# One step for each score tile, squares and scalings that VectorE may take, and another written order, in a fused attention and feed-forward kernel

## The chip, the cores and the metric

The program runs on one core of a Trainium2 chip. The time is the device time of one execution in microseconds (us); the median of three runs of the kernel before is 430.78 us. PE is TensorE, DVE is VectorE, ACT is ScalarE, POOL is GpSimd, and SP is SyncE, whose queue starts most of the transfers.

## The reference, cut to what matters

```python
# q, k, v: (8, 12, 448, 64); w_in: (768, 2048); w_out: (2048, 768)
q_n, k_n = rmsnorm(q, g_q), rmsnorm(k, g_k)          # over the last axis, 64 long
scores = matmul(q_n, k_n.T) / sqrt(64)
attn   = exp(scores - max);  attn = attn / (sum(attn) + 1e-9)
x      = matmul(attn, v)      # heads side by side: (8*448, 768)
h      = x @ w_in
g      = h * clip(h + 3, 0, 6) / 6
out    = g @ w_out            # (3584, 768)
```

## The kernel before, in words

**Units.** The work of the attention is cut into 48 pairs P of two heads, six pairs for each of the 8 batches. A pair goes through these steps. `load` fetches q, k and v of the pair, 256 KB each, by three transfers in SP's queue. `prep` squares q and k (`f_sq`, line 401 on ACT, line 403 on POOL), sums the squares (`f_red`, line 410, DVE), makes the inverse root out of a logarithm and an exponential (`f_ln` and `f_ex`, lines 415 and 418, ACT), scales q and k with it into bf16 (`f_sc`, line 427) and casts v (`f_v`, lines 345 to 351). `trans` transposes the scaled q and k, in PE for the pairs below 13 (line 479) and by a DMA transpose from SP's queue for the rest (line 455). `score` multiplies q by k (line 510), and ACT takes the exponential of a score tile out of PSUM (`f_e`, line 519). `av` multiplies by v (line 531), `finish` divides by the sums (lines 547 and 550) and turns the result into a piece of `xT`, in PE for batches 0 and 1 (line 566) and by a DMA transpose for the rest (line 557).

The feed-forward part has for each batch 16 groups `h` of six matmuls with `w_in` (line 587), each of which needs all six pairs of its batch, an ACT step (line 594) and a DVE step (line 597). For two batches together it has seven groups `y` of 32 matmuls with `w_out` (line 618), evacuated by ACT or DVE and stored. The first two `h` groups of batch 0 are cut into six parts of one matmul each, one part for each pair; every other `h` group is two parts of three. A half of a `y` group is four parts of four matmuls, and part n reads the n-th quarter of `w_out`.

**Score tiles.** A pair has four score tiles of 112 rows by 2 x 448. One tile is two matmuls with 64 rows of weights each, one for each head, and they lie in different halves of the array's rows. There are three places in PSUM for score tiles: `S0` and `S1` in turn, and `X`, which is used for it (the flag `wide`) in pairs from 24 on. `av` accumulates in `X` as well. The two banks `M0` and `M1` serve the `h` and `y` groups.

**Order.** Every step is first recorded in a `Plan` with the engines that could run it. `WAY` names, by step number, which of these engines is taken (0 where nothing stands). The steps are then written out in the order of the list `ORDER`, and `em` ties each instruction to the one before it on its engine. So each engine, and each queue of transfers, runs its steps in exactly that order: a step that waits holds up everything behind it on the same engine. The numbers of time and load in `plan.add` and the values `want` and `since` do not reach the chip; only `WAY` and `ORDER` do.

Before the change one `score` step held the tiles of a group: one tile for pairs below 6, two tiles for pairs 6 to 23, and three, two and three tiles for two pairs from 24 on. A group's matmuls cannot be parted by other work:

```python
def f_s(_):
    for P, t, ps, _ in parts:
        ...
plan.add(pe(0.2 + 0.19 * len(parts)), want, f_s, sorted(reads), [p[3] for p in parts], soon=soon)
```

The squares could be taken by POOL or ACT; the scalings were DVE's for pair 0 and POOL's for the other 47 pairs. The weights are fetched by POOL's queue, four transfers for `w_in` (line 653) and four for `w_out` (line 658), 768 KB each in the type that is stored.

At the start, 120 matmuls on zeros (line 356) keep PE running, and three small ones (line 536) follow each `av` step of the first six pairs.

Of the kernel before, what the change touches and what calls it, by code (L numbers as in the profile page):

```python
# [10 lines left out]
A_MULT = mybir.AluOpType.mult  # L11
# [10 lines left out]
WAY = {53: 1, 63: 2, 67: 1, 68: 1, 69: 1, 78: 1, 83: 1, 84: 1, 95: 1, 101: 1, 126: 1, 132: 2, 157: 1,  # L22
    163: 1, 183: 1, 188: 1, 225: 1, 231: 1, 233: 1, 245: 1, 250: 1, 256: 1, 276: 1, 358: 1, 365: 1, 377: 1,
    388: 1, 400: 1, 424: 2, 429: 1, 446: 1, 453: 1, 458: 1, 460: 1, 487: 1, 500: 1, 505: 1, 516: 1, 518: 1,
    533: 1, 625: 1, 636: 1, 676: 1, 683: 2, 709: 2, 714: 1, 728: 1, 729: 1, 755: 1, 761: 2, 766: 1, 793: 1,
    798: 1, 821: 1, 892: 1, 899: 2, 925: 2, 930: 1, 945: 1, 951: 2, 977: 2, 1003: 2, 1008: 1, 1023: 1,
    1029: 1, 1034: 1, 1061: 1, 1097: 1, 1134: 1, 1148: 1, 1182: 2, 1206: 1, 1212: 1, 1226: 1, 1251: 1,
    1257: 2, 1263: 1, 1398: 1, 1413: 1, 1420: 2, 1426: 1, 1440: 1, 1447: 1, 1453: 1, 1464: 1, 1465: 1,
    1491: 1, 1515: 1, 1516: 1, 1522: 1, 1549: 1, 1555: 1, 1579: 1, 1615: 1, 1620: 1, 1652: 1, 1673: 1,
    1693: 1, 1700: 1, 1706: 1, 1718: 1, 1724: 2, 1744: 1, 1751: 2, 1757: 1, 1781: 1, 1795: 1, 1832: 1,  # L30
    1893: 1, 1921: 1, 1932: 1, 1938: 1, 1958: 1, 1971: 1, 1979: 1, 1980: 1, 1986: 1, 1992: 1, 2057: 1,
    2062: 1, 2093: 1, 2098: 1, 2125: 1, 2145: 1, 2162: 1, 2169: 1}


class Plan:

# [8 lines left out]
    def add(self, ways, want, fn, reads=(), writes=(), load=(), since=0.0, soon=()):  # L49
        i = len(self.ops)  # L50
        self.way[i] = WAY.get(i, 0)
        eng, occ, fin = ways[self.way[i]]
        soon = dict(soon)
        preds = {}

        def after(p, lat):
            preds[p] = max(preds.get(p, 0.0), lat)

        for r in reads:
            if r in self.last:  # L60
                after(*self.last[r])
            self.readers.setdefault(r, []).append((i, fin))
        for w in writes:
            for p in self.readers.get(w, ()):
                if p[0] != i:
                    after(*p)
            if w in self.last:
                after(*self.last[w])
        for w in writes:
            self.last[w] = (i, soon.get(w, fin))  # L70
            self.readers[w] = []
        self.ops.append((eng, occ, fin, want, fn, preds, load, since))
        self.ways.append(ways)
        return i

    def emit(self, order):

        place = {i: n for n, i in enumerate(order)}
        assert len(place) == len(self.ops)
        for i, o in enumerate(self.ops):  # L80
            assert all(place[p] < place[i] for p in o[5])
        for i in order:
            self.ops[i][4](self.ops[i][0])
# [3 lines left out]
    8, 9, 20, 13, 21, 22, 15, 23, 11, 24, 28, 10, 25, 19, 29, 53, 26, 12, 30, 27, 14, 54, 31, 16, 55, 32, 33,  # L87
    34, 17, 58, 35, 56, 36, 83, 37, 92, 38, 78, 59, 39, 60, 40, 57, 62, 41, 18, 69, 42, 43, 44, 61, 45, 93,
    68, 66, 46, 73, 47, 67, 64, 123, 48, 101, 70, 49, 50, 74, 122, 65, 75, 71, 63, 77, 104, 72, 217, 102, 84,
    105, 76, 81, 85, 154, 51, 103, 112, 94, 124, 82, 79, 52, 86, 114, 80, 113, 153, 126, 115, 110, 87, 95,  # L90
    155, 135, 88, 111, 96, 91, 89, 136, 106, 116, 184, 117, 107, 133, 97, 118, 90, 143, 119, 185, 156, 108,
    134, 132, 120, 186, 144, 109, 141, 121, 248, 142, 145, 146, 166, 98, 1, 157, 164, 147, 167, 158, 148, 99,
    165, 174, 163, 149, 215, 137, 150, 159, 172, 100, 125, 387, 138, 151, 175, 127, 0, 139, 216, 173, 218,
    140, 187, 152, 195, 128, 197, 188, 129, 196, 176, 177, 178, 198, 130, 179, 189, 203, 160, 204, 205, 131,
    246, 180, 168, 181, 190, 206, 161, 169, 170, 247, 182, 171, 191, 183, 162, 228, 385, 226, 229, 207, 194,
    208, 386, 201, 227, 199, 192, 209, 416, 202, 210, 200, 236, 211, 234, 225, 212, 237, 230, 414, 219, 213,
    249, 259, 214, 231, 6, 220, 238, 260, 239, 193, 235, 445, 267, 2, 221, 232, 240, 222, 268, 241, 257, 223,
    242, 233, 243, 415, 258, 250, 261, 244, 262, 245, 265, 256, 251, 277, 266, 278, 224, 269, 279, 280, 281,
    443, 252, 396, 388, 253, 397, 263, 270, 271, 264, 255, 272, 398, 285, 286, 273, 287, 274, 288, 254, 289,
    401, 275, 444, 389, 402, 395, 399, 276, 390, 400, 3, 290, 282, 406, 291, 407, 5, 391, 403, 292, 392, 283,  # L100
    472, 405, 394, 297, 284, 298, 404, 393, 293, 299, 408, 294, 417, 502, 300, 425, 295, 418, 305, 426, 296,
    306, 4, 427, 419, 501, 301, 307, 302, 420, 430, 308, 428, 421, 303, 409, 422, 431, 313, 429, 424, 473,
    446, 314, 423, 304, 432, 410, 315, 411, 309, 433, 316, 310, 474, 434, 412, 321, 413, 311, 322, 312, 454,
    323, 531, 447, 435, 455, 436, 324, 317, 456, 448, 318, 329, 319, 503, 475, 459, 449, 457, 320, 450, 437,
    460, 438, 330, 452, 458, 439, 440, 453, 325, 331, 451, 461, 530, 332, 462, 441, 326, 476, 442, 463, 337,
    338, 477, 327, 7, 483, 339, 464, 328, 484, 621, 465, 504, 466, 340, 467, 478, 333, 485, 468, 482, 469,
    486, 345, 479, 487, 480, 488, 346, 489, 470, 622, 534, 490, 347, 471, 491, 334, 348, 481, 493, 492, 494,
    495, 335, 496, 512, 336, 647, 533, 497, 513, 341, 498, 342, 535, 514, 499, 515, 343, 517, 516, 344, 648,
    536, 505, 354, 537, 518, 506, 539, 349, 500, 350, 538, 507, 351, 508, 649, 509, 519, 520, 522, 523, 510,
    355, 521, 356, 511, 524, 541, 544, 625, 525, 542, 526, 527, 543, 357, 699, 540, 352, 358, 635, 624, 528,  # L110
    546, 353, 529, 547, 674, 366, 650, 626, 361, 548, 360, 651, 367, 627, 673, 676, 368, 652, 628, 532, 677,
    549, 632, 700, 633, 550, 630, 678, 551, 552, 369, 634, 629, 553, 362, 679, 554, 675, 370, 637, 653, 545,
    654, 661, 728, 363, 655, 638, 555, 378, 556, 656, 639, 379, 701, 636, 380, 687, 703, 680, 658, 752, 659,
    364, 681, 623, 640, 660, 726, 641, 365, 631, 642, 381, 702, 371, 729, 663, 382, 730, 751, 373, 664, 682,
    374, 665, 704, 375, 731, 889, 732, 684, 662, 705, 727, 685, 561, 643, 686, 562, 644, 645, 376, 706, 372,
    563, 734, 688, 689, 713, 377, 690, 666, 893, 667, 564, 668, 669, 725, 691, 557, 708, 683, 558, 646, 755,
    670, 671, 710, 657, 559, 890, 569, 733, 711, 560, 570, 672, 892, 707, 565, 712, 894, 891, 566, 571, 692,
    739, 693, 567, 694, 572, 695, 895, 915, 715, 896, 568, 716, 577, 696, 709, 578, 753, 717, 573, 383, 714,
    754, 574, 579, 736, 384, 697, 575, 737, 580, 718, 698, 719, 756, 720, 738, 585, 765, 586, 576, 757, 918,
    359, 721, 758, 741, 587, 722, 723, 742, 735, 581, 588, 759, 582, 724, 743, 740, 744, 593, 583, 941, 760,  # L120
    762, 584, 967, 763, 594, 944, 589, 903, 764, 897, 590, 968, 595, 745, 767, 591, 898, 916, 596, 768, 746,
    592, 747, 601, 919, 748, 769, 749, 602, 993, 766, 761, 597, 603, 920, 900, 750, 901, 770, 771, 772, 604,
    969, 773, 902, 598, 774, 775, 994, 970, 609, 921, 599, 899, 610, 922, 776, 924, 600, 905, 611, 908, 906,
    909, 612, 923, 605, 917, 904, 907, 606, 955, 617, 607, 618, 1019, 608, 945, 926, 619, 946, 942, 613, 927,
    910, 943, 911, 928, 620, 614, 996, 912, 929, 781, 947, 913, 948, 615, 997, 931, 925, 1020, 932, 934, 616,
    935, 950, 914, 782, 998, 933, 936, 949, 1021, 777, 783, 937, 999, 784, 778, 1000, 938, 952, 939, 779,
    1146, 1001, 789, 953, 956, 940, 790, 1002, 780, 954, 791, 951, 981, 1148, 971, 785, 1147, 786, 972, 957,
    787, 960, 958, 961, 1197, 788, 792, 1022, 930, 1196, 794, 793, 973, 1149, 959, 795, 1145, 796, 1023, 1150,
# [79 lines left out]
def kernel(  # L208
# [11 lines left out]
    nc = tc.nc  # L220
# [116 lines left out]
    def pool(n, rate):  # L337
        return POOL, 0.02 + n * rate, 0.05 + n * rate
# [443 lines left out]
```

## Time and profile before

| what | value |
|---|---|
| median of three runs | 430.78 us (430.08 to 431.27) |
| span of the profiled execution, first to last instruction | 427.8 us |
| granted TensorE clock | 1.000 |
| PE busy | 415.1 us, 97% |
| ACT, DVE, POOL busy | 296.7, 219.6, 171.1 us |
| transfers | 67.77 MB |

The page gives the span of one execution and not that execution's own time; the median of the runs lies 3.0 us above the span, and this is taken as what lies around it. A row of a group of instructions has the line, the engine, the operation, what is written and read, the shapes and the count; behind the bar stand the busy time in us, the mean of one in ns, and the idle time of the engine just before. A row of the timeline has the start and the length in us, and in brackets how long the engine had been idle and what ended this.

### The profile page before, as it was taken

What the parts mean: (1) busy time and instruction counts of PE and PEld (TensorE: products, weight loads), DVE (VectorE), ACT (ScalarE), POOL (GpSimd) and SP (SyncE); (2) the same over time, 40 slices, a digit from 0 to 9 for tenths busy, and PEclk for the clock granted to TensorE, in tenths of its full rate; (3) what the DMA queues carried; (4) which work ended last, traced back from release to release, by engine and by line L of the source; (5) the groups of instructions that cost most, each with busy time, mean ns of one, the idle gap of its engine ahead of it and who ended that gap; (6) DMA issues with size and microseconds to landing.
All of it is one profiled execution on the core that took longest, in us unless ns stands there. A gap on an engine that the chain in (4) does not pass through costs nothing.

```text
span 427.8 us, 9914 instructions
## 1 busy us (share of the span) xinstructions
PE 415.1 (97%) x3946; PEld 238.6 (56%) x3946; DVE 219.6 (51%) x405; ACT 296.7 (69%) x535; POOL 171.1 (40%) x188
## 2 busy tenths in 40 slices
PE   9678999999999999999999999999999999999996
PEld 8455455555555555555555555555555555655554
DVE  5665776547787965665545454434434332243211
ACT  5999898889998988968757977575575556222221
POOL 2899865874767866255524340312200000000000
PEclk9999999999999999999999999999999999999999
DMA  8999999698799999668565865352413221021113
GB/s 258 349 249 288 242 240 250 149 267 231 197 237 262 229 234 227 187 155 233 136 170 132 215 156 124 75 125 55 93 33 70 50 60 49 11 75 37 38 38 113
DMA packets 98931, 67.77 MB, mean 158 GB/s; under 512 B 53156, under 2 KB 95428, under 8 KB 98884
## 3 DMA queue, kind: packets, MB, share of 16 engines
q1 hardware_dynamic: 93248, 60.50, 54.5%
q0 software_dynamic: 5248, 6.29, 8.4%
q8 instruction: 31, 0.51, 0.5%
q10 hardware_dynamic: 388, 0.34, 0.3%
q14 instruction: 16, 0.13, 0.1%
HBM read 50.23 MB, written 11.01 MB: 143 GB/s over the span
## 4 chain that ended last, share of the span: by engine, by line
PE 90%; ACT 4%; issue 2%; DVE 1%; DMA 1%; POOL 1%; SPq 0%; POOLq 0%
PE M L587 32%; PE M L618 29%; PE X L531 10%; PE S L510 8%; PE S L618 5%; ACT eT L519 2%; PE X L587 1%; DMA qk<-in_k_dram 1%; PE S L587 1%; PE X L510 1%; PE X L618 1%; POOL qks L427 1%; DVE gT L597 0%; SPq L388 0%; ACT ts L594 0%
## 5 line engine op out<-in xcount | busy, mean ns | idle before, releaser
L519 ACT ACTIVATE eT<-S 112x896 bf16<-112x896 f32 x168 | 148.1, 918 | 13.8 <-PE S L510 13.3
L587 PE MATMUL M<-xT,w_in_sb 128*128 128x448 bf16 x714 | 153.2, 353 | 0.8 <-ACT xT L347 0.4
L618 PE MATMUL M<-w_out_sb,gT 128*128 128x384 bf16 x752 | 135.9, 326 | 0.0
L597 DVE SCALAR_TENSOR_TENSOR gT<-ts,M 128x448 bf16<-128x448 f32 x119 | 73.4, 619 | 101.9 <-ACT ts L594 101.7
L427 POOL TENSOR_TENSOR qks<-qk,rs 112x512 bf16<-112x512 f32 x94 | 96.2, 1043 | 65.5 <-DMA T<-qks 31.9
L618 PEld LDWEIGHTS <-gT 128*128 128x128 bf16 x912 | 84.8, 98 | 61.9 <-issue 9.7
L594 ACT ACTIVATE ts<-M 128x448 f32<-128x448 f32 x119 | 64.8, 548 | 61.0 <-PE M L587 59.8
L587 PEld LDWEIGHTS <-w_in_sb 128*128 128x128 bf16 x768 | 69.9, 98 | 65.7 <-issue 10.9
L403 POOL TENSOR_TENSOR sq<-qk 112x512 f32<-112x512 f32 x56 | 57.7, 1041 | 43.4 <-DMA qk<-in_k_dram 18.2
L531 PEld LDWEIGHTS <-eT 112*128 112x128 bf16 x1536 | 57.1, 97 | 18.1 <-issue 8.2
L410 DVE TENSOR_REDUCE ssq<-sq 112x16 f32<-112x1024 f32 (+1 forms) x50 | 57.9, 1172 | 15.8 <-ACT sq L401 11.9
L531 PE MATMUL X<-va,eT 112*128 112x65 bf16 x1536 | 62.3, 194 | 1.0 <-DVE xT L349 0.8
L510 PE MATMUL S<-T 64*128 64x448 bf16 x336 | 47.3, 354 | 2.1 <-ACT eT L519 1.5
L550 DVE TENSOR_TENSOR xn<-X,rd 112x512 bf16<-112x512 f32 x48 | 33.2, 691 | 1.6
L351 POOL CAST va<-vf 112x512 bf16<-112x512 f32 x20 | 12.3, 613 | 41.1 <-PE X L531 38.8
L510 PEld LDWEIGHTS <-T 64*128 64x128 bf16 x384 | 12.8, 94 | 27.9 <-issue 21.0
L401 ACT ACTIVATE sq<-qk 112x512 f32<-112x512 f32 x40 | 24.9, 629 | 4.7 <-DMA qk<-in_q_dram 2.3
L347 ACT COPY y<-M 128x384 f32<-128x384 f32 x26 | 12.5, 481 | 18.4 <-PE M L618 18.1
L547 DVE RECIPROCAL rd<-X 112x8 f32<-112x8 f32 x48 | 9.8, 204 | 28.1 <-PE X L531 27.9
L349 DVE COPY y<-M 128x384 f32<-128x384 f32 x21 | 11.7, 555 | 22.8 <-PE M L618 22.6
L519 ACT ACTIVATE eT<-X 112x896 bf16<-112x896 f32 x24 | 22.1, 923 | 0.0
L618 PE MATMUL S<-w_out_sb,gT 128*128 128x384 bf16 (+1 forms) x128 | 21.8, 316 | 0.0
(58 smaller groups left out, 188.3 us busy)
## 6 DMA issues: line engine op xcount, KB each, us to landing
qk<-in_q_dram SPq DMA_DIRECT2D x47, 256.0 KB, 4.2
qk<-in_k_dram SPq DMA_DIRECT2D x47, 256.0 KB, 4.0
vf<-in_v_dram SPq DMA_DIRECT2D x47, 256.0 KB, 4.8
w_in_sb<-in_moe_w_in_dram POOLq DMA_DIRECT2D x4, 768.0 KB, 12.7
w_out_sb<-in_moe_w_out_dram POOLq DMA_DIRECT2D x4, 768.0 KB, 14.5
out_dram<-y SPq DMA_DIRECT2D x7, 336.0 KB, 2.8
out_dram<-y SPq DMA_DIRECT2D x8, 288.0 KB, 2.7
out_dram<-y SPq DMA_DIRECT2D x8, 240.0 KB, 3.4
```

Of the source, the lines that this page charges most:

```text
L401: em(nc.scalar.square(out=sq[:, i], in_=x))
L403: em(nc.gpsimd.tensor_tensor(out=sq[:, i], in0=x, in1=x, op=A_MULT))
L410: em(nc.vector.tensor_reduce(out=ssq[:, s].rearrange("p i n -> p (i n)"), in_=sq[:, s].rearrange("p i (n d) -> p (i n) d", d=D), axis=AX_X ...
L427: em((nc.vector if e == DVE else nc.gpsimd).tensor_tensor(out=qks[:, i].rearrange("p t h d -> p h t d"), in0=qk[:, i].rearrange("p h (t d) ...
L510: em(nc.tensor.matmul(out=ps[:, a, 0:S], lhsT=qkT[r, S + t * TP:S + t * TP + 128], rhs=qkT[r, 0:S], start=True, stop=True))
L519: em(nc.scalar.activation(out=eT[:, t, 0:S2].rearrange("p (a s) -> p a s", a=2), in_=ps[0:TP, :, 0:S], func=EXP, bias=0.0, scale=1.0))
L531: em(nc.tensor.matmul(out=X_ps[:, a, i * E1:(i + 1) * E1], lhsT=eT[:, t, c:c + 128], rhs=va[:, a, t, :], start=(t == 0 and i == 0), stop=( ...
L550: em(nc.vector.tensor_tensor(out=xn[:].rearrange("p i a d -> p a i d"), in0=xv[:, :, :, 0:D], in1=rd[:].unsqueeze(3).to_broadcast([TP, 2, ...
L587: em(nc.tensor.matmul(out=ps[:, 0:S], lhsT=w_in_sb[:, kt, f * 128:(f + 1) * 128], rhs=xT[:, kt, :], start=(kt == 0), stop=(kt == NKT - 1)))
L594: em(nc.scalar.activation(out=ts[:], in_=ps[:, 0:S], func=RELU, bias=0.5, scale=1.0 / 6.0))
L597: em(nc.vector.scalar_tensor_tensor(out=gT[:, f, e * S:(e + 1) * S], in0=ts[:], scalar=1.0, in1=ps[:, 0:S], op0=A_MIN, op1=A_MULT))
L618: em(nc.tensor.matmul(out=ps[:, 0:nc0], lhsT=gT[:, f, i * 128:(i + 1) * 128], rhs=w_out_sb[:, f, c0:c0 + nc0], start=(f == 0), stop=(f == ...
```

## The change

The kernel computes the same. Four things differ:

- `score` takes one tile, so each of the 192 tiles is a step that can be placed by itself.
- A square may also be taken by DVE, and a scaling by DVE or POOL for any pair. The new `WAY` puts 27 of the 96 squares on DVE (before none), 46 on POOL (56) and 23 on ACT (40); and 41 of the 96 scalings on DVE (2) and 55 on POOL (94). Casts of v, copies and evacuations are handed out anew too: POOL casts v 28 times (20), ACT 8 (12), DVE 12 (16); DVE evacuates `y` 32 times (25), ACT 25 (32).
- `ORDER` is another list throughout.
- The model's numbers in `plan.add` change. They have no effect on the program but through `WAY` and `ORDER`.

```diff
-    def score(slots, want):
-        parts = [(P, t, *((X_ps, ("X",)) if wide else sbank())) for P, t, wide in slots]
+    def score(P, t, wide, want):
+        ps, res = (X_ps, ("X",)) if wide else sbank()
+        qkT, eT, n = T_r[P % NT], eT_r[P % NE], P % NE
...
-        plan.add(pe(0.2 + 0.19 * len(parts)), want, f_s, sorted(reads), [p[3] for p in parts], soon=soon)
...
+        plan.add(pe(0.192), want, f_s, [(("T", P % NT), i) for i in range(2)], [res], half=True)
+        plan.add([act(S2)], want, f_e, [res], [("e", n, t)])
...
-            score(slots, gw)
+            for slot in slots:
+                score(*slot, gw)
...
-                    em(nc.gpsimd.tensor_tensor(out=sq[:, i], in0=x, in1=x, op=A_MULT))
-            plan.add([pool(n, 1.9e-3), act(n, 0.03)][::-1 if P in SQ_ACT else 1], want, f_sq,
+                    em((nc.vector if e == DVE else nc.gpsimd).tensor_tensor(out=sq[:, i], in0=x, in1=x, op=A_MULT))
+            plan.add([pool(n, 1.9e-3), act(n, 0.03)][::-1 if P in SQ_ACT else 1] + [(DVE, 0.62, 0.7)], want, f_sq,
...
-            plan.add([(DVE, 0.75, 0.85) if P == 0 else pool(n, 1.95e-3)], want + 0.01, f_sc,
+            plan.add([(DVE, 0.75, 0.85), pool(n, 1.95e-3)][::1 if P == 0 else -1], want + 0.01, f_sc,
...
-            plan.add([(POOL, 0.8, 3.0)], -20.0, f_o, [], [("w_out", c)], load=(4.8, 150), since=AT_OUT[c])
+            plan.add([(POOL, 0.8, 3.0)], -20.0, f_o, [], [("w_out", c)], load=(4.2,), since=AT_OUT[c])
```

In the program that this gives, as its instructions stand on each engine: PE has the same 3945 matmuls; the score matmuls stand in 97 unbroken runs (before 88), and 76 of the runs (before 72) come after the first `w_in` matmul. In POOL's queue the last transfer of `w_out` stands behind 38 squares and scalings, 10 casts and 7 other weight transfers (before 36, 6 and 7), and behind 14 squares and scalings that the list gives to DVE ahead of it (before 2). In SP's queue 46 loads stand ahead of the first DMA transpose (before 52).

## The prediction

> **What bounds the kernel now.** I read the busy table first, then PE's waits with times, then the table of windows. PE is busy for nearly all of the span, and its table of waits from 50 us to the end has two entries of 0.2 us each. So the windows have to say where PE's idle time lies:
>
> ```profile
> PE 415.1 (97%) x3946; PEld 238.6 (56%) x3946; DVE 219.6 (51%) x405; ACT 296.7 (69%) x535; POOL 171.1 (40%) x188
> 0.00:45.00 45.00, 36.35 (x566) 26.87 (x567) 27.52 (x58) 37.85 (x73) 34.51 (x47) 1.00 1.06 284
> 45.00:75.00 30.00, 29.41 (x294) 16.10 (x292) 20.80 (x36) 27.04 (x52) 19.15 (x20) 1.00 1.10 243
> 75.00:424.40 349.40, 349.37 (x3092) 195.61 (x3088) 171.32 (x312) 231.52 (x410) 117.39 (x122) 1.00 0.55 136
> ```
>
> A window's row has the window, its length, the busy time of PE, PEld, DVE, ACT and POOL, the clock, the share of the DMA engines and GB/s. PE idles for 8.65 us before 45 us, 0.59 us until 75, and 0.03 us in the next 349. After 75 us nothing can be won but matmul work itself. The two things that can move the end are how early PE has the pairs of batch 0 and then runs without a gap, and whether the matmuls take longer in another order. Nearly 7 us of the 36.35 are the 120 matmuls on zeros (57 ns each), so PE has more room at the start than the row says. The DMA share is above 1 until 75 us: the transfers are full there, which is the second limit.
>
> The price of a score run is in PE's timeline, in a stretch without a wait:
>
> ```profile
> 297.46 1.30 PE L587 MATMUL M<-xT,w_in_sb 128*128 128x448 bf16 x6
> 298.69 0.55 PE L510 MATMUL S<-T 64*128 64x448 bf16 x4
> 299.18 0.82 PE L618 MATMUL M<-w_out_sb,gT 128*128 128x384 bf16 x4
> ```
>
> Six `h` matmuls start 189 ns apart elsewhere, 1.13 us in all; here the scores start after 1.23, so going in costs 0.10. The four score matmuls hold PE for 0.49 us where two tiles at 0.19 would be 0.38: going out costs 0.10 as well.
>
> The start's clock is ACT, 97% to 98% busy from 10 to 30 us in the windows of ten. Its last exponential of pair 5 begins at 38.24, and with `av`, the division, a transposition and a copy PE gets the last piece of `xT` of batch 0 at 43.53:
>
> ```profile
> 38.24 0.92 ACT L519 ACTIVATE eT<-S 112x896 bf16<-112x896 f32 x1
> 43.53 0.54 PE L587 MATMUL M<-xT,w_in_sb 128*128 128x448 bf16 x2 [0.42 <-ACT xT L347]
> ```
>
> The other limit is the last transfer of `w_out`, read by the thirteenth `y` matmul:
>
> ```profile
> 61.90 0.80 POOL L658 DMA_DIRECT2D w_out_sb<-in_moe_w_out_dram x1
> 71.78 2.48 PE L618 MATMUL M<-w_out_sb,gT 128*128 128x384 bf16 x13
> DMA to landing us min/median/max: 10.9/14.5/18.1
> ```
>
> Issued at 61.90, it lands at 72.8 by the shortest of the three figures, about 1 us before PE asks at 73.9. It is hidden now, but only just.
>
> **Score tiles apart.** There are 97 score runs instead of 88, not 192, for the new list mostly puts tiles side by side again. Nine more at 0.20 us are 1.8 us of PE. Five of them stand ahead of the first `w_in` matmul, where PE idles: nothing, and 1.0 us if that idling is gone. Four stand in the closed stretch: +0.8. Adding up the starts from one matmul to the next over the whole list, with 189 ns for `h`, 162.5 for `y`, 31 for `av` and 49 for a transposition, the PE work left after batch 0's last piece of `xT` is 380.06 us, before 379.66. So +0.4 counts from that mark on; the remainder is ahead of it.
>
> **The start.** From the first exponential to pair 5's last one, ACT's list loses four squares, one copy or scaling of `T`, one copy of `xT` and one cast of v, and gains one exponential and one logarithm with its exponential. At their pitches (0.81 for the large exponential, 0.52 for a square, cast or scaling, 0.43 for a copy, 0.24 for the small pair) the new list is 20.25 + 0.52 + 0.52 + 0.43 + 1.68 = 23.4 us; the old one comes to 25.8 and took 27.6, so 1.8 us of waits. The first exponential is at 11.53 now, because ACT was squaring until then; q and k of pairs 0 and 1 now come first in SP's queue, and following squares, sums, scaling, transposition and copy gives some 10.1. The floor is 10.1 + 23.4 = 33.5, plus 2.1 for the way from the last exponential to PE: 35.6. With the old waits it is 37.4. A ceiling is 43.5, nothing won. I take 39.0, since the list puts eight squares and scalings on DVE ahead of that mark, and T's copies queue behind them (pair 1's behind two), so every wait there reaches the score tiles. That is 4.5 us earlier.
>
> The row for such a step is the only one in which DVE has two inputs in SBUF:
>
> ```profile
> L427 DVE TENSOR_TENSOR qks<-qk,rs x2: 677/893/1109, 7.1 to 8.2; 112x512 bf16<-112x512 f32 x2
> 7.08 0.61 POOL L351 CAST va<-vf 112x512 bf16<-112x512 f32 x1 [2.33 <-DMA vf<-in_v_dram]
> ```
>
> The first of the two, at 7.12, took 1109 ns while POOL's cast ran; the second, with POOL idle, 677. So one costs DVE 0.68 to 1.11 us. What POOL loses the trace does not show; I bound it by none and by 0.62, the pitch of the DVE step. [...]
>
> **The weights.** Ahead of the last transfer of `w_out` POOL has 38 squares and scalings at 1.00 us, 10 casts at 0.57 and 7 issues at 0.88: 49.9 us. It starts on them near 6.5, so the issue is at 56.4 if POOL never waits. Before, the same sum (36, 6, 7) from 3.7 gives 49.3 against 61.9, so 12.6 us of waits. In the new order I find one sure wait, pair 8's scaling behind pair 5's third exponential (1.5 us): 58. The 14 DVE steps in front of it add up to 8.7: about 66. I take 62, the middle, where it is now as well. Landing is then 72.9. PE, without a gap from 39.0, has 31.8 us of work to the thirteenth `y` matmul and would ask at 70.8: a wait of 2.1, where today there is none.
>
> **Later on.** The other 54 squares and scalings of DVE stand behind that. Counted at these pitches (1.14 us for a sum, 0.54 for a `gT` step), DVE's work goes from 8 to 18 us up to 14 to 18 us in each 20 us of PE's work between 60 and 260. Today a window with DVE busy for 9.38 of 10 us (140 to 150) has no idle PE, so I take little: 0.5 us for late `gT` steps, bounds 0 and 3. SP's loads of 0.37 to 0.5 us in its queue and the DMA transposes moved past each other cost nothing while the DMA share is 0.55; if that cover fails, pair 13's DMA transpose (3.5 us to landing) is late for its scores, and with it the DVE step that scales it and the steps queued behind that. The tail, 3.5 us from the last matmul to the last store, stays.
>
> **Sum.** -4.5 (start) + 0.4 (score runs) + 2.1 (w_out) + 0.5 (DVE) = -1.5. The profiled span goes from 427.8 to 426.3, and with 3.0 us around it to 429.3. What a measurement of this kernel can tell from no change is 0.3%, 1.3 us, so this forecast is only just a gain.
>
> **Rivals.** *No exclusion to speak of:* POOL issues at 58, the weights land at 69, batch 0 is ready at 37.4, and PE asks at 69.2. -6.1 + 0.4 + 0.3 = -5.4: 425.4. For it: ACT is relieved where it is 97% busy. Against it: the 1109 ns. Chance 0.25.
>
> *POOL held up by DVE* (the slower side): the last `w_out` transfer is issued at 66, lands at 77, and PE stands at the thirteenth `y` matmul for 6 us: -4.5 + 0.4 + 6.1 + 1.5 = +3.5: 434.3. It decides from an issue at 63 on for no gain (landing 74, a wait of 3.6 with the 0.5), and from 65 on for a loss that can be measured. For it: POOL is 94% to 100% busy from 20 to 50 us, so there is nothing to catch up with. Chance 0.27.
>
> *The start isn't won at all*, because DVE, with some 28 us of work ahead of that mark, takes ACT's place as the limit: the copies of `T` come as late as now, +0.4 + 0.5 = +0.9: 431.7. Chance 0.10. The forecast itself has 0.38.
>
> **The numbers.** The forecast's own range is 427.5 to 431.5, and half of it lies beyond 0.3% below. Faster: 0.25 + 0.21 and a little from the rivals' near edges, 0.49; same: 0.21; slower: 0.30. The range reaches the first rival, 425.2, and most of the second, 433.5.
>
> **What would show it.** Right: PE's idle time before 45 us falls by some 4 us; an idle gap of about 2 us before the early `w_out` matmuls, released by a DMA; DVE's two-input squares near 0.9 us on average; no idle after 80 us. The first rival shows these at 0.68 and no gap; the second a gap of 6 and POOL steps over 1.04 us. It is wrong if PE has idle time after 80 us in the sum of more than 3 us, or if batch 0's last piece comes after 42.

## The result, and the profile after

The changed kernel takes 448.85 us (median of six runs, 446.28 to 450.13) against 430.08 us for the kernel before beside it: a ratio of 1.042, with a 95% interval of 1.039 to 1.045. The prediction was 429.3 with a range from 425.2 to 433.5. The profiled execution took 450.13 us with a span of 448.3, so 20.5 us of span have to be found. It is the slowest of the six and has the lowest mean clock of them (0.974, the others 0.979 to 0.993), so its trace shows more half speed than most of them had.

From the page of the changed kernel, the span, the busy table and the row of the granted clock (one digit for each 11.2 us):

```profile
span 448.3 us, 9887 instructions
PE 428.5 (96%) x3946; PEld 247.2 (55%) x3946; DVE 276.1 (62%) x475; ACT 280.1 (62%) x501; POOL 139.8 (31%) x147
PEclk9887969999999999999999999999999999999998
```

The work moved as the change says: DVE from 219.6 to 276.1 us, POOL down by 31, ACT by 17. The row of the clock is new. Before it had no digit under 9; now TensorE is, ahead of the tail, at half speed in three stretches of the clock's records, 15.7 to 19.1, 29.4 to 39.6 and 60.1 to 66.9 us: 20.5 us, in lengths of 3.41, 10.24 and 6.83. There the `h` matmuls start 373 ns apart instead of 189.

The windows of the changed kernel, with the columns as before:

```profile
0.00:45.00 45.00, 38.31 (x486) 28.39 (x487) 32.83 (x60) 30.98 (x58) 31.30 (x40) 0.85 0.87 241
45.00:80.00 35.00, 30.45 (x315) 17.46 (x312) 30.68 (x43) 24.07 (x48) 24.89 (x27) 0.90 0.87 175
80.00:443.40 363.40, 359.48 (x3153) 201.34 (x3150) 212.58 (x374) 224.75 (x397) 83.61 (x81) 1.00 0.57 138
```

Before 45 us PE executes 486 matmuls in place of 566; ACT, the old limit of the start, is busy for 31.0 us where it was 37.9. From 45 to 80 us PE idles for 4.6 us, and after 80 us for 3.9, where it had 0.03. Two rows of the timeline and one of the last transfers of `w_out` answer to those of before:

```profile
48.61 0.74 PE L583 MATMUL M<-xT,w_in_sb 128*128 128x448 bf16 x3
86.82 1.46 PE L614 MATMUL M<-w_out_sb,gT 128*128 128x384 bf16 x8
77.98 1.55 POOL L654 DMA_DIRECT2D w_out_sb<-in_moe_w_out_dram  x2
```

The second matmul of the first row reads batch 0's last piece of `xT`, at 48.8 us (before 43.53, forecast 39.0). The thirteenth `y` matmul, inside the second row, is at 87.5 (before 73.9). The last transfer of `w_out` goes out at 78.8, 17 us later than assumed, and no matmul waits for it, because PE is later still.

For a ledger I use the starts of PE's matmuls: whatever one start comes later than its normal distance (189 ns for `h`, 162.5 for `y`, 31 for `av`, 49 for a transposition, 95 ns more ahead of and after scores) is idle time or, in the stretches at half speed, the clock's. This counts gaps that the windows hide behind overlapping matmuls (0.9 us after 80 us in the kernel before, 8.7 now).

| from before to after, us of span | |
|---|---|
| to 45 us: idle 10.4 to 6.9, half speed 0 to 4.9 | +1.4 |
| 45 to 80 us: idle 1.2 to 5.3, half speed 0 to 2.5 | +6.6 |
| after 80 us: idle 0.9 to 8.7 | +7.8 |
| the nine more score runs | +1.4 |
| the matmuls on zeros at the start, and the tail | +3.3 |

PE's table of waits shows what released the long gaps:

```profile
PE M L583 <- DVE gT L593: 5.8, 8, 3.4
PE S L509 <- DVE T L349: 2.0, 1, 2.0
```

DVE, each time. The longest gap is PE's second row here; the rows of DVE and POOL from the same microseconds say why:

```profile
57.65 0.57 PE L509 MATMUL S<-T 64*128 64x448 bf16 x4
61.67 2.40 PE L583 MATMUL M<-xT,w_in_sb 128*128 128x448 bf16 x6 [3.45 <-DVE gT L593]
```

```profile
54.95 1.21 DVE L410 TENSOR_REDUCE ssq<-sq 112x16 f32<-112x1024 f32 x1
56.19 4.89 DVE L403 TENSOR_TENSOR sq<-qk 112x512 f32<-112x512 f32 x1
61.01 0.61 DVE L593 SCALAR_TENSOR_TENSOR gT<-ts,M 128x448 bf16<-128x448 f32 x1
```

```profile
55.39 1.04 POOL L427 TENSOR_TENSOR qks<-qk,rs 112x512 bf16<-112x512 f32 x1
56.39 1.03 POOL L403 TENSOR_TENSOR sq<-qk 112x512 f32<-112x512 f32 x1
57.39 1.03 POOL L427 TENSOR_TENSOR qks<-qk,rs 112x512 bf16<-112x512 f32 x1
58.38 0.60 POOL L351 CAST va<-vf 112x512 bf16<-112x512 f32 x1
58.95 1.03 POOL L427 TENSOR_TENSOR qks<-qk,rs 112x512 bf16<-112x512 f32 x1
59.93 0.60 POOL L351 CAST va<-vf 112x512 bf16<-112x512 f32 x1
62.82 1.04 POOL L403 TENSOR_TENSOR sq<-qk 112x512 f32<-112x512 f32 x1 [2.29 <-DVE ssq L410]
```

The square of pair 13 starts on DVE at 56.19. POOL ends the step it is in and goes on with five more without a pause, at their full pace, until 60.53; the square's row ends 0.55 us after that. PE waits for the `gT` step behind it, whose ACT step had ended at 57.0. While PE stands, the clock falls (at 60.07), and the matmuls up to 66.9 take twice as long.

All the two-input steps of DVE, and POOL's squares beside them, from the groups of the page:

```profile
L403 DVE TENSOR_TENSOR sq<-qk 112x512 f32<-112x512 f32 x27 | 28.7, 1070 | 1.1 <-DMA qk<-in_q_dram 1.0
L427 DVE TENSOR_TENSOR qks<-qk,rs 112x512 bf16<-112x512 f32 x41 | 35.4, 869 | 4.8 <-ACT rs L418 4.8
L403 POOL TENSOR_TENSOR sq<-qk 112x512 f32<-112x512 f32 x46 | 52.4, 1146 | 74.5 <-DVE gT L593 32.9
```

The means lie inside the 0.68 to 1.11 that the prediction used, and so does their sum: 64.1 us for 68 steps, where 0.68 each would be 46.2. What the prediction did not have is single steps above this range at places where PE had nothing else to do. The square at 56.19 is the longest; a scaling at 13.84 stands in the same way ahead of a copy of `T`:

```profile
13.84 1.52 DVE L427 TENSOR_TENSOR qks<-qk,rs 112x512 bf16<-112x512 f32 x1
15.28 0.38 DVE L349 COPY T<-M 128x448 bf16<-128x448 bf16 x1
15.71 0.56 PE L509 MATMUL S<-T 64*128 64x448 bf16 x2 [1.96 <-DVE T L349]
```

### The profile page after: what moved, and what is told of

Same layout as the page of the kernel before. It is cut to its first block, busy times and chain, and to the rows that moved or that the text cites. A ratio compares the mean times of both kernels' runs of the same rounds, so it can differ in the third digit from the quotient of the medians.

```text
span 448.3 us, 9887 instructions
## 1 busy us (share of the span) xinstructions
PE 428.5 (96%) x3946; PEld 247.2 (55%) x3946; DVE 276.1 (62%) x475; ACT 280.1 (62%) x501; POOL 139.8 (31%) x147
## 4 chain that ended last, share of the span: by engine, by line
PE 66%; DVE 13%; DMA 7%; issue 5%; ACT 4%; SPq 2%; POOL 1%; ACTq 0%; DVEq 0%; POOLq 0%
PE M L583 23%; PE M L614 19%; PE X L527 8%; PE S L509 6%; PE S L614 4%; DVE sq L403 3%; DVE gT L593 2%; ACT eT L514 2%; DVE qks L427 2%; DVE ssq L410 2%; DMA qk<-in_q_dram 2%; DVE xn L546 2%; SPq L388 1%; DMA out_dram<-y 1%; PE X L583 1%
## 5 line engine op out<-in xcount | busy, mean ns | idle before, releaser
L583 PE MATMUL M<-xT,w_in_sb 128*128 128x448 bf16 x714 | 160.5, 355 | 7.3 <-DVE gT L593 5.8
L614 PE MATMUL M<-w_out_sb,gT 128*128 128x384 bf16 x752 | 138.6, 326 | 0.0
L427 POOL TENSOR_TENSOR qks<-qk,rs 112x512 bf16<-112x512 f32 x55 | 61.8, 1132 | 77.7 <-ACT rs L418 60.2
L527 PEld LDWEIGHTS <-eT 112*128 112x128 bf16 x1536 | 64.4, 99 | 26.4 <-issue 8.8
L403 POOL TENSOR_TENSOR sq<-qk 112x512 f32<-112x512 f32 x46 | 52.4, 1146 | 74.5 <-DVE gT L593 32.9
L527 PE MATMUL X<-va,eT 112*128 112x65 bf16 x1536 | 71.3, 196 | 2.5 <-ACT xT L347 1.1
L509 PE MATMUL S<-T 64*128 64x448 bf16 x336 | 51.6, 365 | 2.0 <-DVE T L349 2.0
L427 DVE TENSOR_TENSOR qks<-qk,rs 112x512 bf16<-112x512 f32 x41 | 35.4, 869 | 4.8 <-ACT rs L418 4.8
L351 POOL CAST va<-vf 112x512 bf16<-112x512 f32 x28 | 20.9, 751 | 50.6 <-PE X L527 41.9
L347 ACT COPY y<-M 128x384 f32<-128x384 f32 x22 | 10.4, 478 | 33.5 <-PE M L614 33.3
L403 DVE TENSOR_TENSOR sq<-qk 112x512 f32<-112x512 f32 x27 | 28.7, 1070 | 1.1 <-DMA qk<-in_q_dram 1.0
L514 ACT ACTIVATE eT<-X 112x896 bf16<-112x896 f32 x24 | 21.9, 914 | 10.8 <-PE X L509 10.4
L543 DVE RECIPROCAL rd<-X 112x8 f32<-112x8 f32 x48 | 9.8, 204 | 28.5 <-PE X L527 28.3
```

Of the source, the lines that this page charges most:

```text
L351: em(nc.gpsimd.tensor_copy(out=out, in_=in_))
L403: em((nc.vector if e == DVE else nc.gpsimd).tensor_tensor(out=sq[:, i], in0=x, in1=x, op=A_MULT))
L427: em((nc.vector if e == DVE else nc.gpsimd).tensor_tensor(out=qks[:, i].rearrange("p t h d -> p h t d"), in0=qk[:, i].rearrange("p h (t d) ...
L509: em(nc.tensor.matmul(out=ps[:, a, 0:S], lhsT=qkT[r, S + t * TP:S + t * TP + 128], rhs=qkT[r, 0:S], start=True, stop=True))
L514: em(nc.scalar.activation(out=eT[:, t, 0:S2].rearrange("p (a s) -> p a s", a=2), in_=ps[0:TP, :, 0:S], func=EXP, bias=0.0, scale=1.0))
L527: em(nc.tensor.matmul(out=X_ps[:, a, i * E1:(i + 1) * E1], lhsT=eT[:, t, c:c + 128], rhs=va[:, a, t, :], start=(t == 0 and i == 0), stop=( ...
```

## The experiments

"Theory A" in the first expectations below is that the change loses because DVE's two-input steps and POOL's steps shut each other out, and by the clock that falls in the stalls; "Theory B", that the new order loses by itself. The runs show that such steps hold each other up (in the changed kernel a square of DVE took up to 4.89 us where it takes 0.68 with POOL idle, and a POOL step up to 1.59 where the kernel before has 1.04), not where they meet. Three marks of each trace are used: batch 0's last transposition, the thirteenth `y` matmul (called y13), and the time from y13 to the end of the span. The times are medians of all runs, the marks are those of one profiled execution each; the ratio is to the kernel before on the same chip.

| kernel | us | ratio, 95% interval | last transposition | y13 | y13 to end |
|---|---|---|---|---|---|
| before | 430.08 | 1 | 42.70 | 73.94 | 353.9 |
| after | 448.85 | 1.039 to 1.045 | 48.06 | 87.47 | 360.8 |
| after, one SBUF input | 438.25 | 1.014 to 1.021 | 41.77 | 75.89 | 360.2 |
| the same, more buffers | 435.14 | 1.004 to 1.017 | 41.14 | 74.55 | 357.0 |
| after, DVE's steps on ACT and POOL | 440.44 | 1.019 to 1.028 | 42.43 | 77.87 | 360.0 |
| before's order, new engines | 443.64 | 1.025 to 1.034 | 46.95 | 78.69 | 362.8 |
| the same, one SBUF input | 441.35 | 1.020 to 1.028 | 47.27 | 78.47 | 360.6 |
| after, pair 13's square on ACT | 445.70 | 1.025 to 1.039 | 45.31 | 79.30 | 364.5 |
| after, more buffers | 450.49 | 1.039 to 1.050 | 46.55 | 86.12 | 360.5 |
| new start, old rest | 441.04 | 1.020 to 1.026 | 47.32 | 86.16 | 354.0 |
| old start, new rest | 451.20 | 1.042 to 1.052 | 42.46 | 84.11 | 366.3 |
| new start without DVE's steps, old rest | 434.82 | 1.006 to 1.012 | 43.26 | 77.53 | 354.2 |

**The second input taken away.** Same list, same engines, but no DVE square or scaling reads two tensors from SBUF:

```diff
-    em(nc.vector.tensor_tensor(out=sq[:, i], in0=x, in1=x, op=A_MULT))
+    em(nc.vector.tensor_scalar(sq[:, i], x, 1.0, None, A_MAX, A_ADD, accum_out=junk_t[0:TP]))
...
-    em(nc.vector.tensor_tensor(out=..., in0=..., in1=rs[...].to_broadcast(...), op=A_MULT))
+    em(nc.vector.tensor_scalar(..., ..., rs[:, i, 0:1], None, A_MULT, A_ADD, accum_out=junk_t[0:TP]))
```

> The changed kernel with the same order and the same engines, but each of DVE's 27 squares and 41 scalings in a form with one SBUF input: the larger of x and 1 in place of x*x, and a multiplication by one column of rs in place of all eight, so the squaring and seven of eight factors are left out on DVE. Theory A (DVE's two-input steps and POOL's steps shut each other out of SBUF, and nothing else is wrong): these DVE steps fall from 1070 and 869 ns to 0.65 to 0.80 us including the read of the accumulator, POOL's steps go back to 1.04, no PE gap of 2 us is left, the clock stays at 1.00, and the time is 424 to 430 us. Theory B (the order itself is too tight, with tiles apart and DVE fuller): the gaps behind DVE stay, 440 us or more.

It took 438.25: neither. DVE's scalings take 0.74 us on average (0.87 in the changed kernel), and POOL's squares are back to their old time:

```profile
L408 POOL TENSOR_TENSOR sq<-qk 112x512 f32<-112x512 f32 x46 | 47.4, 1040 | 70.1 <-DMA qk<-in_q_dram 32.9
L433 DVE TENSOR_SCALAR_CACHE_REDUCE qks<-qk,rs 112x512 bf16<-112x512 f32 x41 | 30.4, 741 | 5.7 <-ACT rs L423 4.9
```

No step is held (the longest takes 0.75 us), the clock does not fall before the end in this execution, and y13 comes at 75.9 instead of 87.5. So of the 13.5 us lost up to y13, 11.6 go with the second input, the clock included. (Two of the other three executions had a mean clock of 0.992, which is some 7 us of half speed, so not every one is free of it.) After y13 little changes (360.2 against 360.8): 6.3 of the other 6.9 us are lost without the second input as well.

**No DVE steps at all.** The 27 squares to ACT, 40 of the 41 scalings to POOL, the list as it is.

> The changed kernel's order, with DVE's 27 squares given to ACT and 40 of its 41 scalings to POOL (one of pair 0 stays on DVE). Theory A: POOL's steps are back at 1.04 us, no DVE step lasts over 1.3 us, PE's idle time after 80 us falls from 8.7 to below 3 us, while the start gets later, since 40 us of scalings come back to POOL, 10 of them ahead of batch 0's end: 432 to 442 us. Theory B (the order is too tight whatever the engines): PE's idle time after 80 us stays at 7 us or more, 445 us or more.

At 440.44 the time is what Theory A says and the rest after y13 (360.0) is what Theory B says: the list loses late even with nothing for POOL to collide with.

**The new engines in the old order.**

> The order of the kernel before, with every square and scaling on the engine that the changed kernel gives it; all else as before. Theory A: DVE's squares and scalings last 0.9 to 1.1 us on average with single ones of 2 us and more, PE idles for 5 us and more after 45 us where it idled 1.2, and the time is 436 to 450 us. Theory B (the order is at fault, not the engines): 429 to 433 us, as the order before left DVE idle nearly half of the time.

443.64 is a time that Theory A gave, with 6.8 us of half speed. But the steps are not those of Theory A: DVE's squares and scalings took 0.77 and 0.83 us on average, none over 1.5. The same with one SBUF input in each DVE step tests the reason. If the second input made the whole loss, the time would come back to that of the kernel before:

> The order of before with the new engines for squares and scalings, as in the run that took 443.6 us, but each square and scaling on DVE with one SBUF input (max(x, 1) and a product with one column of rs, so its values are others). [...] Rival (DVE has simply too much to do at the wrong times, whatever its inputs): 438 or more, idle after 80 us 7 or more.

441.35: the rival. Here the second input is worth 2.3 us of the 12.5, and the clock was at half speed for 6.8 us again, so stalls and half speed come with one input too (PE's longest wait, 2.8 us until 28.3, was for a `T` from DVE). What costs is the place of the steps in DVE's queue, as these rows of this kernel show; the `h` matmuls that need the `gT` step at 304.13 stood for 0.74 us:

```profile
301.95 0.74 DVE L432 TENSOR_SCALAR_CACHE_REDUCE qks<-qk,rs 112x512 bf16<-112x512 f32 x1
302.74 0.68 DVE L476 TENSOR_SCALAR_CACHE_REDUCE T<-T,gp_t 128x448 bf16<-128x448 bf16 x1
303.46 0.75 DVE L432 TENSOR_SCALAR_CACHE_REDUCE qks<-qk,rs 112x512 bf16<-112x512 f32 x1
304.13 0.61 DVE L603 SCALAR_TENSOR_TENSOR gT<-ts,M 128x448 bf16<-128x448 f32 x1
```

**One step.** Only the first square of pair 13 changes its engine (`512: 2` becomes `512: 1` in `WAY`).

> The changed kernel with one engine changed: the first square of pair 13 (the DVE step at 56.19 us that lasted 4.89) on ACT, where a square takes 0.52. If that one step makes PE's stall of 3.8 us at 57.86 and the 6.8 us of half speed after it (2.45 us of PE's time): 442 to 445 us, no PE gap over 1.5 us between 55 and 70, no half speed after 50. Rival (another wait is next in line there, or the lost time is given back later): 447 to 449.5, and a gap of 2 us or more released by another step.

445.70, 0.7 us beyond the first answer, and both answers hold in part. No gap over 0.9 us is left between 50 and 70 us, there is no half speed there, and the way from the last transposition to y13 takes 34.0 us instead of 39.4: 5.4 won, the 3.3 of the stall and most of the 2.5 of the clock. But from y13 on it takes 3.6 us more than the changed kernel: PE, no longer late, waits for `gT` 8 times for 4.8 us in all after 50 us, in gaps of 1.1 us at most.

**The same square, a little later.** Two small reciprocals on DVE ahead of it.

> The changed kernel with two reciprocals of 128 x 1 values (unused) on DVE just ahead of the first square of pair 13, so that it starts some 0.2 to 0.4 us later, when POOL is early in a step instead of 0.24 us from the end of one. If 4.89 us come from the moment at which the step begins (it lost its turn five times in a row): the step takes 1.0 to 1.8 us, PE's stall at 57.86 falls to 1.5 or less, 443 to 446 us. If a run of POOL steps without a pause keeps DVE out whenever it begins: the step still ends near 61, 4.3 to 4.7 us long, 448 to 450.

```profile
56.24 0.35 DVE L405 RECIPROCAL junk_t<-gp_t 128x1 f32<-128x1 f32 x2
56.51 4.75 DVE L406 TENSOR_TENSOR sq<-qk 112x512 f32<-112x512 f32 x1
```

The step began 0.27 us later, 0.10 us before the end of POOL's step instead of 0.24, and again stood until POOL paused. For the step it was the second answer; the time, 453.85 us, is beyond both. In this run another square, at 27.68, was held for 3.92 us over three scalings and a cast of POOL. But the start early in a POOL step, which the first answer asked for, was not reached, so it is not refuted. In most places DVE gets its turn after one POOL step, and POOL's next one then lasts 1.49; with the new start the square of pair 13 was held until POOL paused, in all six programs that had it on DVE there.

The traces of all runs bear on the question. In them 237 two-input steps of DVE began while a POOL step ran. The 148 that began 0.5 us or more before its end lost only that one turn and took 1.54 us at most. All 20 that lost more began in its last 0.5 us, and the eight that stood for 3.9 to 4.95 us began 0.10 to 0.37 us before its end. A late start is not enough: 69 others began as late and lost one turn only. What tells these apart stays open.

**Buffers.** Traces of the one-input kernel showed DVE's `xn` step waiting, with `gT` queued behind, for the DMA transpose that still read its buffer (two buffers of `xn`, three of `y`):

```profile
155.88 0.69 DVE L557 TENSOR_TENSOR xn<-X,rd 112x512 bf16<-112x512 f32 x1 [2.04 <-DMA xT<-xn]
156.49 0.61 DVE L604 SCALAR_TENSOR_TENSOR gT<-ts,M 128x448 bf16<-128x448 f32 x1
```

```diff
-    NQK, ..., NXN, NXT, NTS, NY = 5, 5, 2, 4, 3, 4, 4, 2, 2, 2, 2, 3
+    NQK, ..., NXN, NXT, NTS, NY = 5, 5, 2, 4, 3, 4, 4, 2, 3, 2, 2, 5
```

"Without the port" in the next expectation means with one SBUF input in each of these DVE steps; no run shows a port.

> The one-input kernel of before (the new list, every DVE square and scaling with one SBUF input: max(x, 1) and a product with one column of rs, so its values are others), with three buffers of xn instead of two and five of y instead of three. Theory C (what is left of the loss without the port comes from buffers that DMAs hold: DVE steps that write xn or y wait for the DMA transpose and the store that read the buffer, with the gT steps queued behind): 433 to 436 us, PE's idle time after 80 us under 5 us instead of 7.6, no gap of PE released by xn. Theory D (the buffers don't matter; the new list has gT, T or a DMA too late by itself): 437 to 439, and the gaps stand where they stood, put down to another step.

435.14 (433.33 in the profiled execution), with these windows after 80 us, of the kernel without and with the buffers:

```profile
80.00:431.20 351.20, 347.59 (x3001) 194.55 (x2999) 203.93 (x416) 215.32 (x381) 71.36 (x78) 1.00 0.56 138
```

```profile
80.00:426.60 346.60, 345.25 (x2985) 193.46 (x2984) 202.55 (x414) 214.89 (x379) 71.46 (x78) 1.00 0.56 138
```

PE's idle time falls from 3.61 to 1.35 us by the windows, from 7.6 to 5.1 by the starts; two gaps, 0.7 us in sum, are still released by `xn`. By these two executions Theory C holds for 3.2 us of the rest after y13. With no DVE squares the same buffers gave:

> The new list with DVE's squares on ACT and 40 of its 41 scalings on POOL, as in the run that took 440.4 us, with three buffers of xn instead of two and five of y instead of three. Theory C (buffers held by DMAs): 435 to 438 us, PE's idle time after 80 us under 5 instead of 7.4. Theory D: 439 to 442. Neither theory expects it below the kernel before: its PE work alone is 3.5 us longer.

436.94, a time that Theory C gave (434.54 to 441.62; the profiled execution is the one at 441.62, with 10.2 us of half speed at the start, so its trace is not read here and PE's idle time not known). And in the changed kernel itself:

> The changed kernel with three buffers of xn instead of two and five of y instead of three, nothing else. If the buffers held by DMAs cost what they cost where DVE's squares had one input (4.5 us of span): 443 to 446 us, PE idle after 80 us near 6 instead of 8.7. If the slow DVE steps hide that wait, so that the two don't add: 447 to 449.

450.49, the second answer, a little over it: no gain, 360.5 us after y13. Where DVE's two-input steps are held up by POOL's (1.07 and 0.87 us on average in the changed kernel, up to 4.89), the buffers are not what is late.

> The kernel before with three buffers of xn and five of y. Theory C says that these buffers are short only in the new list: PE's idle time after 80 us is 0.9 in all here, so 429.3 to 430.8 us, no difference that can be told. If its list too waits for them in places that PE's gaps don't show: 428 or less.

431.27 against 431.02, ratio 0.997 to 1.002. The old list does not need them.

**Two halves.** What belongs to the start and what to the rest? One list up to the first `y` matmul, the other after it (`ORDER` and `WAY` alone are joined):

> The new list and its engines up to the first y matmul (507 of the 2294 steps), then the remaining steps in the order of before with the engines of before. In the changed kernel PE takes 365.1 us from the 96th h matmul to the end, before 356.8. Theory L (these 8.3 us belong to the later part of the new list itself): 441 us (439 to 443), PE idle after 80 us 2 or less. Rival (they are a late effect of the start: loads, squares and transpositions pushed back there and never caught up): 446 or more.

```profile
90.22 1.46 PE L609 MATMUL M<-w_out_sb,gT 128*128 128x384 bf16 x8 [1.06 <-DMA w_out_sb<-in_moe_w_out_dram]
```

441.04, as Theory L says to the microsecond. The rest takes 354.0 us, as long as in the kernel before, although its start is 12 us late. The one long gap is a wait for `w_out`, 1.06 us: the very wait that the prediction had put at 2.1.

> The reverse: the order and engines of before up to the first y matmul (499 steps), then the remaining steps of the new list with its engines. Theory L: 438 us (436 to 440), PE idle after 80 us 7 or more. Rival: 433 or less.

451.20, beyond both: the joint itself makes PE stand for 3.2 and 2.7 us between 72 and 79, with DVE's sum of squares waiting 2.9 us for a square that POOL had still to do, and the clock falls there. After it the loss is there again (from y13 366.3 us). It speaks for Theory L, but for no size.

> As the kernel with the new start and the old rest, but in the start DVE's squares are ACT's and its scalings but one POOL's. From the two runs that each did one of these, theory L: 440.4 less 7.5, 433 (431 to 435), no better than the kernel before, since the start without DVE's steps reaches the 96th h matmul at 73.6 and before at 71.0. Rival: 437 or more.

434.82, inside what Theory L gave. It is still slower than the kernel before, and no version tried beats that one.

**The clock by itself.** Twice I filled PE's stalls with matmuls on zeros. The first put them into the bank `S0`:

> The changed kernel with matmuls on zeros put into PE's queue ahead of the three places where PE stood still for 2 us and more (40, 20 and 40 of 57 ns, into the score place S0). The stops themselves stay. Theory A1 (the stops have a second price, since the clock is halved after them for 20.5 us in all): the clock stays at 1.00 and the time falls by 6 to 9 us to 440 to 443. Rival (half clock costs nothing, because PE waits for DVE in these stretches anyway): 447 to 449.

452.90, and useless for the question: the half speed fell to 6.8 us, but PE stood for 6.2 us at 25.5. In this run a square of DVE at 24.22 was held for 4.95 us; ACT waited for the sum behind it, and the zeros until ACT, behind that, had read the tile in `S0`. The second wrote columns that nobody reads:

> The changed kernel with matmuls on zeros, 29 ns each, put into the four long stalls of PE: 60 ahead of pair 1's first score tile (stall of 2.3 us), 30 ahead of its first av step (1.3), 50 ahead of its transposition of xn (2.1), 100 ahead of the first part of f = 6 of batch 0 (3.8). They write the columns 448 to 511 of a bank that nobody reads. If the halved clock has a price of its own: 441 to 446 us, half speed for 7 us or less instead of 20.5. If it is hidden behind the waits for DVE and ACT: 447 to 450 with as little half speed. If the clock isn't set by idle PE at all: half speed stays near 20 us.

452.73, with 6.8 us of half speed. At the two gaps that `T` and `gT` end, the zeros waited for the same DVE step as the matmuls behind them, and so only added their 1.7 and 2.9 us. The last transposition came 1.1 us earlier with 10.2 us less of half speed ahead of it. Nothing on the price follows from either kernel.

What does say something are four executions whose programs have the same steps in the same order on PE, DVE, ACT and POOL up to 45 us: with 3.4, 6.8, 10.2 and 13.7 us at half speed there (square on ACT, more buffers, new start with old rest, after), the last transposition came at 45.3, 46.6, 47.3 and 48.1. (A fifth, the one with the second held square, had 6.8 us and came at 48.2.) That is some 0.27 us for each microsecond at half speed, or an estimate of 3.7 of the 6.3 us between the changed kernel and its one-input form at that mark. It is argued from runs that were made for other questions, not shown by taking the clock's fall away.

The mean clock of every execution gives a second estimate. The records of the changed kernel's trace have the clock at 1 or at half and nothing between, so twice what the mean lacks to 1, times the span, is the time at half speed: 23.0 us there, the 20.5 and 2.5 in the tail. For the other executions it is an estimate by the same sum. In the six executions of the changed kernel this lies between 6 and 23 us, with spans from 444.5 to 448.3: some 0.17 us of span for each microsecond. Over the 73 executions of all 16 kernels tried, each taken against the mean of its own kernel, it is 0.31. By these two, the 20.5 us of half speed cost an estimated 3.5 to 6.4 us of span. This too is argued, since a longer stall can both cost time and lower the clock.

## Why the prediction was wrong

**The price of a DVE step** is the step that failed first. "One costs DVE 0.68 to 1.11 us", from two instructions at 7 us, had as its upper end one turn lost to POOL. The measured range is 0.68 to 4.89. The working then spread this price over the steps, by which only the work of an engine grows; what a held step does to the matmul that waits behind it had no term. With one SBUF input in each of these steps the kernel takes 10.6 us less (448.85 to 438.25). The longest step, 4.89 us in front of a `gT` step for which PE had no other work, is 3.2 of them: that is what the kernel won with it on ACT. The others, such as the one at 13.84, and the half speed after the stalls were not taken apart further. The rival with a loss let the exclusion act through POOL and so through `w_out`. POOL did lose (its squares rose from 1.04 to 1.15 us, its scalings from 1.04 to 1.13), but no matmul waited for `w_out`: PE waited for `T`, `xn` and `gT` out of DVE's queue. The rows at 56.19 go beyond the one turn of that upper end: DVE was out for the end of one POOL instruction and five whole ones.

**The clock** had no term at all. 7.4 us of PE's time were lost to it in the profiled execution, up to 80 us, of which an estimated 3.5 to 6.4 reach the end. The prediction had shown the clock at 1.00 in all its windows and did not ask what would become of it with stalls of 2 to 3.5 us.

**The start, -4.5**, would have failed without the held steps and the half speed too. It was a sum over ACT's list with ACT's waits of before. The list was right, the waits were not: by the prediction's own sum (23.4 us of ACT's work from the first exponential to the end of pair 5's last one) ACT waits for 4.4 us there in the one-input kernel and for 11.0 in the changed one, where it had waited for 1.8 of 27.6 before, because it waits for PE's score tiles and PE for `T`, `xn` and `xT` out of DVE's queue (gaps of 1.1 and 1.6 us at 13.9 and 24.3). The last transposition came 0.9 us earlier than before at best with two buffers, not 4.5. "A ceiling is 43.5, nothing won" was taken for a bound; it was none, since DVE could also make the start later, and 48.8 came.

**Later on, +0.5 (bounds 0 and 3).** Measured: 6.9 us from y13 to the end. The reason given, that a window with DVE busy for 9.38 of 10 us had no idle PE, was no measure of room: the new engines in the old order lose 8.9 us after y13 as well. The second input has 0.6 of the 6.9, and the buffers, once these steps have one input, 3.2. The 0.6 is small, it seems, because PE comes late in the changed kernel: with pair 13's square on ACT PE is at y13 at 79.3 and then takes 364.5 us, 4.3 more than with one input everywhere. Which of the list's many moves make up the last 3.1 was not tried; in that kernel, the one with more buffers, 22 short gaps that `gT` releases come to 2.1 us. The tail, which was to stay at 3.5 us, is 4.7 in the changed kernel and 4.3 in this one.

**Score runs, +0.4.** 1.4 over the whole by the ledger, where nine runs at the 0.19 of its two distances would be 1.7; those ahead of the first `w_in` matmul were not hidden, since PE's idle time there shrank.

**The weights, +2.1.** Right in kind and hidden in the end: no wait in the changed kernel, where PE came to the thirteenth `y` matmul 16.7 us later than assumed, and 1.06 us in the run with the old rest.

**The time around the span.** 3.0 us was the median less the span; an execution's own time lies 1.8 above its span here (450.13 and 448.3). Of the two signs that were to prove the forecast wrong, idle time over 3 us after 80 us and a last piece after 42, both came.

## What to carry to other kernels

When a step moves to an in-order engine, price what stands behind it at that place, not its mean duration: ask which matmul waits for the next result of that engine, and how long the step can be held at worst. A two-input vector step from SBUF beside a GpSimd that does not pause can lose far more than one turn: 4.89 us here for a step of 0.68. And a list of steps that keeps PE fed is fitted to its engines: the new engines in the old order cost 12.5 us here, and most of it with one SBUF input in each DVE step as well.

## What the runs showed of the hardware

- A DVE `tensor_tensor` with both inputs in SBUF was held until GpSimd, which ran steps without a pause, had ended five more (4.89 us in the changed kernel at 56.19, where its two-input squares and scalings took 0.68 to 0.69 in the 30 cases with POOL idle). All 20 such steps that lost more than the running GpSimd step began in its last 0.5 us; the 148 that began earlier in one took 1.54 us at most. With one input in each of these steps, in the same list, none took over 0.75 us.
- PE's clock fell to half for 3.41, 6.83 or 10.24 us after gaps much shorter than that: it fell beside idle gaps of 1.96, 1.73 and 3.45 us in the changed kernel, and did not after gaps of 1.74 and 1.98 us in the kernel without DVE's steps. The first of these waits, 1.73 us in the run that joins this start to the old rest, was followed by 3.41 us at half speed. So gaps under 2 us were followed by half speed in some executions, and gaps as long were not in others.
